# A fused mLSTM, trilinear mixture and Mish mixture: the Mish by ScalarE's own function in two reads of a bank

## The chip, the cores and the metric

One NeuronCore of a Trainium2 chip runs one program. The metric is the device time of one execution in microseconds (us).

## What is computed

Three stages follow one another. An mLSTM attention over 768 steps (2 batches, 8 heads, 40 columns a head) gives 1536 tokens of 320 numbers. The first mixture is `((x @ w1) * (x @ w2)) @ w3 @ w_out` with 1024 inner columns. The second is this, with 2048 inner columns:

```
h = x @ w_in                                                   # 1536 x 320 @ 320 x 2048
sp = np.where(h > 20.0, h, np.log1p(np.exp(np.minimum(h, 20.0))))
g = h * np.tanh(sp)                                            # Mish of h
out = g @ w_out                                                # 2048 x 320
```

The weights arrive as float64. Every product is made from a high and a low part of each operand, three matmuls for one.

## The kernel before

The tokens are handled in three blocks of 512. Inner columns go in tiles of 128, so that a block has 8 tiles in the first mixture and 16 in the second; there are 24 and 48 tiles in all.

**Order.** No loop runs as written. Each step is a node (`Work.add`, L57) with an engine, a due time, a length, the nodes that it needs and the buffers that it takes. `Work.run` (L79) plays this through once while the program is built: on a free engine the nodes that can start within a slack (`s_pe`, `s_act`, `s_dve`, `s_pool` in `TUNE`, L30) of the earliest are compared, and the one that is due first is issued. The order that comes out is fixed in the program, engine by engine. While TensorE has nothing to do before the attention's end, the planner puts in products without a use (`keep_warm`, L365, tile psz); `w0n` of them stand at the start, and the attention's units below `warm` have four each (two in `S_`, two in `Y`).

**Attention.** Twelve units (`add_unit`, L371). Node E, the exponents of a unit, takes one of NW = 3 places named w, which Y of an earlier unit frees (L521). S needs E of its unit and Y of the unit `ahead` before it (L524).

**Weights.** 80 pieces of up to 128 x 384 (`add_piece`, L271), in one fixed order: w1 and w2 (16), w_out of the first mixture (8), w3 (24), the first half of the second mixture's w_out (8, "wo2"), its w_in (16, "wi"), the rest of wo2 (8). A piece is loaded by SyncE's queue; ScalarE takes the magnitude (`mag`, L285); VectorE clamps and joins the words (L289, L293, L298, L303); ScalarE writes the high part (`hi`, L308); GpSimd subtracts for the low part (`lo`, L311, by the helper in L211). There are NF = 5 places f, each held from `mag` to `lo`, and NRAW = 4 places for the loads. From the 17th piece on, `hi` waits for the attention's end (the node `late`); that of a wi piece waits for the product of the third block whose weights lie in its place.

**First mixture.** For each tile two products A and B (L756, L764) of eight matmuls with 512 columns (`mm320`, L742), then Ph, Pl, and X1 (eight matmuls of 512, L778). After a block's last X1, X1l (L814) writes the input of the second mixture. w3 @ w_out is made beforehand (node W, L714).

**Second mixture**, `add_second`, L833. H (L837) is eight matmuls of 512 columns into a bank. Then, for each tile of 128 x 512:

- He, L841: the bank is copied to h, by ScalarE for the first 18 tiles (`he_act`), by VectorE for the other 30.
- Hm, L848, VectorE: u = min(h, 20). Hx, L851, ScalarE: exp.
- G, L907, ScalarE, for two tiles at a time (`GRP`): Ln of both, Tanh of both, with a table load before each pair.
- gm, L854: u = u * h. gh, L857: the high part. gl, L861: the low part. All three are VectorE's.
- O (L865): four times three matmuls of 320 columns into four banks that collect over the 16 tiles of a block. After a block's last O four VectorE copies and four DMAs write its rows (L879).

H of a tile needs its wi piece, X1l of its block and the last W (L887). It can write its bank when He of the tile that had the bank is done. O needs gl and its wo2 piece.

Of the kernel before, what the change touches and what calls it, by code (L numbers as in the profile page):

```python
# [10 lines left out]
F32 = mybir.dt.float32  # L11
F32R = mybir.dt.float32r
# [4 lines left out]
# numbers of buffers  # L17
NRAW = 4
NF = 5
# [6 lines left out]
NUH = 22  # L26
NG_ = 3
GRP = 2
# where the streams of work stand in the order
TUNE = dict(  # L30
    s_pe=0.21, s_act=0.25, s_dve=0, s_pool=0.02, warm=5, ahead=6, w0n=10, he_act=18, a0=132.2, ap=2.52,
    a_ld=-24.1, e_e=289.88, e_s=231.89, e_r=475.63, rb=6, g_ld=-373.09, o_1=-239.57, o_2=520.41, c_ld=-47.15,
    c_wo=548.73, cp_wo=0.032, p0=141.8, pp0=6.543, c_12=-449.5, w0=-140.23, wp=0.004, t_0=-366.73,
    c_w3=-109.65, p1=-597.93, pp1=0.013, p2=-192.0, pp2=621.703, x0=337.71, x_p=-433.57, x1=51.37, x2=-134.49,
    xp=0.002, c_o2=449.63, cp_o2=0.01, c_wi=511.67, c_o3=121.71, m0=987.19, mp0=0.005, mp=1.376, m_o=15.52,
    m_g=228.41, m_t=218.91,
)

# the magnitudes of float32 as the high words of float64, read as float32
# [4 lines left out]
class Work:  # L44
    """Orders the work of the engines: nodes with what they depend on, the places that they take and how long they
    are thought to last; on a free engine the node that is due first comes next."""
# [3 lines left out]
    TABLE = 1.3  # L50
    WINDOW = 3.4133
# [27 lines left out]
    def run(self, t0, fill=None):  # L79
# [15 lines left out]
        def place_of(takes, got):  # L95
            """the place of a list that is free first, or None if none is known to be"""
# [13 lines left out]
        while left:  # L110
# [65 lines left out]
def kernel(  # L176
# [69 lines left out]
    # places of 2 KiB in each partition, the first of them from the start  # L246
# [22 lines left out]
    pieces = []  # L269

    def add_piece(due, lead, width, loads, outs, takes=(), gates=()):  # L271
        """outs: functions that give the tiles of the high and the low part, in the places that takes names"""
# [37 lines left out]
        def low():  # L310
# [4 lines left out]
        add_node(("mag", n), "ACT", due - 4, 0.41 * e, mag, [("load", n), ("mag", n - 1)],  # L315
                 [(places("f", NF), [("lo", n)])])
# [8 lines left out]
    def cols_loads(w, ft):  # L325
        """128 columns of a matrix with 384 rows"""
# [28 lines left out]
    # the factors of the exponents, whose rows are high and low parts of 16 rows of gates each  # L355
# [4 lines left out]
    def load_rows(dst, src, u):  # L360
        """the rows of a unit, all heads of one time step side by side"""
# [3 lines left out]
    def keep_warm(n):  # L365
        """products without a use: the tensor engine's clock falls when its array has little to do"""
# [4 lines left out]
    def add_unit(u, due):  # L371
# [10 lines left out]
        def ld_qk():  # L382
            """the columns of a unit, the heads in pairs at partitions 0 and 64"""
# [137 lines left out]
        node("E", "PE", -K["e_e"], 0.87, E, [("lb", int(c > 0)), ("rb", c), ("E", u - 1)],  # L521
             [at("dw"), at("dw"), (places("w", NW), [("Y", u), ("vw", u)])])
        node("dw", "ACT", -K["e_e"] + 1, 0.96, dw, [("E", u)], table=["exp"])
        node("S", "PE", -K["e_s"], 1.75 + wl, S_, [("ld_qk", u), ("E", u), ("Y", u - K["ahead"])], [at("wg"), at("wg")], warm=wl)  # L524
        node("wg", "DVE", -3, 1.2, wg, [("S", u), ("dw", u), ("vw", u)])
        if c > 0:
            node("I", "PE", -2, 0.87, inter, [("ld_qk", u), ("st", u - B), ("rb", c)],
# [8 lines left out]
        node("Y", "PE", 0, 1.75 + wl, Y, [("wg", u), ("ld_kv", u)], [at("cb")], warm=wl)  # L536
# [5 lines left out]
        node("X", "PE", 3, 0.33, X, [("xo", u)], [at("Xl")], warm=0.0)  # L542
# [25 lines left out]
    def start():  # L568
        G = B * H
        # they stand where the activations come later; the rows of the gates eight times, those of sixteen at 32 n used  # L570
# [37 lines left out]
        def part(c0, c1):  # L608
            """the gates of some chunks: what the exponentials are made of"""
# [93 lines left out]
    def add_w3(i, due, due_c):  # L703
# [30 lines left out]
        add_node(("W", i), "PE", due, 0.406 * n, W,  # L734
# [17 lines left out]
    def add_first(kb, ft, due, due_x):  # L752
# [43 lines left out]
        add_node(("A", i), "PE", due, 1.72, A, [("lo", n1), ("A", i - 1), *units], [(MM if kb == NBLK - 1 else MM1, [("Ae", i)])])  # L796
        add_node(("Ae", i), "ACT", due + 1, 0.48, Ae, [("A", i)], [(ZA, [("Ph", i), ("Pl", i)])])
        add_node(("B", i), "PE", due + 1, 1.72, Bp, [("lo", n2), ("A", i), ("B", i - 1)], [(MM if kb == NBLK - 1 else MM1, [("Be", i)])])
# [4 lines left out]
        add_node(("X1", i), "PE", due_x, 1.72, X1, [("Pl", i), ("Wl", ft), ("X1", i - 1), ("late",)],  # L803
                 [(XB, [("X1l", kb)])] * 3 if ft == 0 else [])

        if ft == KF1 - 1:
# [17 lines left out]
            add_node(("X1h", kb), "ACT", due_x + 1, 1.45, X1h, [("X1", i), *mine], [(places("z", 1, 19), [("X1l", kb)])])  # L824
            add_node(("X1l", kb), "DVE", due_x + 2, 3.0, X1l, [("X1h", kb)])

# [1 line left out]
    NT = NBLK * KF2  # L828
    UH = places("z", NUH, 34 - NUH)
# [3 lines left out]
    def add_second(i, due):  # L833
# [7 lines left out]
        def He():  # L841
            t["u"], t["h"] = z_slot("u"), z_slot("h")
            if i < K["he_act"]:
                nc.scalar.copy(t["h"], t["ps"])
            else:
                nc.vector.tensor_copy(out=t["h"], in_=t["ps"])

        def Hm():  # L848
            nc.vector.tensor_scalar_min(out=t["u"], in0=t["h"], scalar1=20.0)  # L849

        def Hx():  # L851
            nc.scalar.activation(out=t["u"], in_=t["u"], func=AF.Exp)  # L852

        def gm():  # L854
            tt(nc.vector, t["u"], t["u"], t["h"], mult)

        def gh():  # L857
            t["gh"] = z_slot("gh").bitcast(F32R)
            nc.vector.tensor_copy(out=t["gh"], in_=t["u"])
# [19 lines left out]
        def out_rows(j):  # L879
# [5 lines left out]

        g = i // GRP
        add_node(("H", i), "PE", due, 1.73, Hp, [("lo", wi_n[ft]), ("X1l", kb), ("H", i - 1), ("W", KC * NC3 - 1)],  # L887
                 [(MM, [("He", i)])])
        uh = (UH, [("gl", i)])
# [11 lines left out]
        if end:  # L901
            takes = [(places("z", 4), [])] * 4
# [115 lines left out]
```

## Time and profile before

| | |
|---|---|
| median of three runs | 475.64 us (474.4 to 475.76) |
| span of the profiled execution, first to last instruction | 478.8 us |
| TensorE matmuls busy | 456.2 us (95%), 2490 instructions |
| VectorE busy | 399.6 us (83%) |
| ScalarE busy | 295.8 us (62%) |
| GpSimd busy | 127.7 us (27%) |
| chain that ended last, shares of the span | TensorE 63%, VectorE 19%, issue 7%, ScalarE 6% |

The profile is of one other execution; the page gives no time for it besides its span, which lies 3.2 us above the median of the runs. The granted clock is a share of full speed: 1.00 is TensorE's level of 2.4 GHz, 0.50 the one of 1.2 GHz. A matmul that waits in TensorE's pipeline counts as busy, so a busy TensorE can still be one at half its clock.

### The profile page before, as it was taken

The page shows a single profiled execution, that of the slowest core. Times are in us where ns is not written, and L with a number is a line of the kernel's source. Part 1 is how long each engine was busy: PE and PEld are TensorE (multiplying, and loading weights), DVE is VectorE, ACT ScalarE, POOL GpSimd, SP SyncE. Part 2 cuts the span into 40 slices and gives each one's busy share as a digit, 9 for nine tenths or more (in the row PEclk, how much of TensorE's full clock was granted, in tenths as well). Part 3 has the DMA queues.
Part 4 walks back from the last instruction along what each step waited for, and adds up shares of the span by engine and source line. Part 5 has one row for each costly group of instructions (what it writes and reads, how often), then busy time and mean ns, then how long its engine had stood idle before and what let it go on. Part 6 is the DMA issues. An engine that isn't in the chain of part 4 may idle for free.

```text
span 478.8 us, 7146 instructions
## 1 busy us (share of the span) xinstructions
PE 456.2 (95%) x2490; PEld 391.3 (82%) x2490; DVE 399.6 (83%) x809; ACT 295.8 (62%) x513; POOL 127.7 (27%) x141
## 2 busy tenths in 40 slices
PE   6999899899899999999999998987999999999997
PEld 4777788788787798988888886776887889999996
DVE  5988996998969668777698886999599988878874
ACT  7453245423226542244355649997799899999990
POOL 3345264452245222232212221226241100000000
PEclk9669655958979999999999999989899999999999
DMA  7915454443412332233323332324120000001001
GB/s 215 288 53 161 149 172 139 124 126 94 126 34 88 120 111 88 89 93 93 98 60 120 100 100 67 100 73 115 50 82 1 27 30 0 1 1 56 0 2 55
DMA packets 31828, 41.93 MB, mean 88 GB/s; under 512 B 2160, under 2 KB 25968, under 8 KB 31792
## 3 DMA queue, kind: packets, MB, share of 16 engines
q1 hardware_dynamic: 31792, 41.48, 28.5%
q8 instruction: 19, 0.31, 0.3%
q14 instruction: 17, 0.14, 0.1%
HBM read 39.50 MB, written 1.97 MB: 87 GB/s over the span
## 4 chain that ended last, share of the span: by engine, by line
PE 63%; DVE 19%; issue 7%; ACT 6%; POOL 2%; DMA 1%; SPq 1%; POOLq 0%; DVEq 0%; ACTq 0%
PE pso L874 12%; PE psh L747 9%; PE psa L747 8%; PE psb L747 7%; PE psw L721 6%; PE psY L471 4%; DVE f L298 3%; PE psS L422 2%; DVE f L289 2%; DVE f L303 2%; PE psz L369 2%; PE psx L788 2%; PE psx L789 2%; PE psx L787 2%; POOL wil L211 2%
## 5 line engine op out<-in xcount | busy, mean ns | idle before, releaser
L747 PE MATMUL psh<-hs,wih 128*128 128x512 f32 x144 | 57.4, 399 | 0.0
L747 PE MATMUL psh<-hs,wil 128*128 128x512 f32 x144 | 49.5, 398 | 3.1 <-POOL wil L211 3.1
L289 DVE TENSOR_SCALAR f<-f 128x384 f32<-128x384 f32 (+2 forms) x80 | 36.8, 463 | 14.0 <-ACT f L285 13.7
L303 DVE SCALAR_TENSOR_TENSOR f<-raw,f 128x384 int32<-128x384 int32 (+2 forms) x80 | 47.0, 592 | 1.0
L285 ACT ACTIVATE f<-raw 128x384 f32<-128x384 f32 (+2 forms) x80 | 41.5, 524 | 10.2 <-DMA raw<-in_w_dram 5.7
L298 DVE SCALAR_TENSOR_TENSOR f<-raw,f 128x384 int32<-128x384 int32 (+2 forms) x80 | 46.7, 589 | 0.9
L874 PE MATMUL pso<-wo,gh 128*128 128x320 f32 x192 | 42.6, 310 | 0.0
L211 POOL TENSOR_TENSOR th<-f,th 128x384 fp32r<-128x384 f32 (+1 forms) x24 | 23.6, 984 | 61.7 <-ACT th L308 51.6
L211 DVE TENSOR_TENSOR u<-u,h 128x512 f32<-128x512 f32 x48 | 35.1, 746 | 4.9 <-ACT u L911 4.9
L747 PE MATMUL psh<-ls,wih 128*128 128x512 f32 x96 | 38.4, 400 | 0.0
L211 DVE TENSOR_TENSOR gl<-u,gh 128x512 fp32r<-128x512 f32 x48 | 32.7, 686 | 4.9 <-PE pso L874 4.2
L747 PEld LDWEIGHTS psh<-hs,wil 128*128 128x128 f32 x144 | 27.7, 193 | 9.5 <-POOL wil L211 3.6
L293 DVE TENSOR_SCALAR f<-f 128x384 int32<-128x384 int32 (+2 forms) x80 | 34.2, 434 | 1.1
L471 PEld LDWEIGHTS psY<-kv,w 128*128 128x128 f32 x192 | 33.6, 256 | 1.5 <-DVE w L211 0.2
L874 PEld LDWEIGHTS pso<-wo,gh 128*128 128x128 f32 x192 | 32.6, 188 | 1.5 <-issue 0.4
L874 PE MATMUL pso<-wo2h,gl 128*128 128x320 f32 x96 | 30.8, 320 | 3.0 <-DVE gl L211 3.0
L747 PE MATMUL psa<-hs,w12h 128*128 128x512 f32 x72 | 30.4, 422 | 3.1 <-DVE hs L211 2.1
L471 PE MATMUL psY<-kv,w 128*128 128x41 f32 x192 | 33.3, 337 | 0.1
L308 ACT CAST th<-f 128x384 fp32r<-128x384 f32 (+1 forms) x24 | 11.5, 480 | 35.3 <-DVE f L303 23.9
L852 ACT ACTIVATE u<-u 128x512 f32<-128x512 f32 x48 | 28.9, 624 | 5.9 <-DVE u L849 5.6
L211 POOL TENSOR_TENSOR wil<-f,wih 128x384 fp32r<-128x384 f32 x16 | 21.5, 1356 | 41.0 <-ACT wih L308 41.0
L747 PEld LDWEIGHTS psh<-hs,wih 128*128 128x128 f32 x144 | 27.8, 193 | 5.0 <-ACT wih L308 0.2
(137 smaller groups left out, 1250.6 us busy)
## 6 DMA issues: line engine op xcount, KB each, us to landing
raw<-in_w_dram SPq DMA_DIRECT2D x32, 384.0 KB
raw<-in_w_out_dram SPq DMA_DIRECT2D x24, 320.0 KB
raw<-in_w_in_dram SPq DMA_DIRECT2D x16, 384.0 KB
kv<-in_kv_dram SPq DMA_DIRECT2D x12, 324.0 KB
qk<-in_qk_dram SPq DMA_DIRECT2D x24, 160.0 KB
raw<-in_w_dram SPq DMA_DIRECT2D x8, 256.0 KB
sg<-in_o_gate_dram SPq DMA_DIRECT2D x12, 160.0 KB
out_dram<-yo SPq DMA_DIRECT2D x12, 160.0 KB
```

The lines of the kernel that those rows point to most:

```text
L211: return eng.tensor_tensor(out=o, in0=a, in1=b, op=op)
L285: nc.scalar.activation(out=t["f"].bitcast(F32), in_=t["raw"][:, :, 1].bitcast(F32), func=AF.Abs)
L289: nc.vector.tensor_scalar(out=ff, in0=ff, scalar1=HI_MIN, scalar2=HI_MAX, op0=ALU.max, op1=ALU.min)
L293: nc.vector.tensor_scalar(out=f, in0=f, scalar1=3, scalar2=0x3FFFFFFF, op0=ALU.logical_shift_left, op1=ALU.bitwise_and)
L298: nc.vector.scalar_tensor_tensor(out=f, in0=t["raw"][:, :, 1], scalar=-0x40000000, in1=f, op0=ALU.bitwise_and, op1=ALU.bitwise_or)
L303: nc.vector.scalar_tensor_tensor(out=f, in0=t["raw"][:, :, 0], scalar=29, in1=f, op0=ALU.logical_shift_right, op1=ALU.bitwise_or)
L308: nc.scalar.copy(t["h"], t["f"].bitcast(F32))
L471: nc.tensor.matmul(ps[:, h * VW:(h + 1) * VW], lhsT=t["w"][:, h, :], rhs=t["v"][:, h, :], start=True, stop=True)
L721: nc.tensor.matmul(ps, lhsT=t[a][:, c * 128:(c + 1) * 128], rhs=wo[b], start=(c0 + c + s == 0), stop=(c0 + c == KC - 1 and s == 2))
L747: nc.tensor.matmul(ps, lhsT=a, rhs=b, start=(n == 0), stop=(n == len(seq) - 1))
L852: nc.scalar.activation(out=t["u"], in_=t["u"], func=AF.Exp)
L874: nc.tensor.matmul(ps, lhsT=t[a][:, sl], rhs=wo[b], start=(ft == 0 and n == 0), stop=(ft == KF2 - 1 and n == 2))
```

## The change

The second mixture's Mish comes from one ScalarE function. It reads the bank of H twice: `Mh` writes the high part directly (the output type rounds), `Mu` writes the full value, and VectorE's gl subtracts. He, Hm, Hx, G, gm and gh go, with their places. The magnitude of the 32 pieces of the second mixture's weights goes from ScalarE to VectorE, as a bit mask. H now waits for the last B, not for the last W. Lengths in the planner and all of `TUNE` are new; the planner lengthens VectorE's nodes by 1.12. Comments that the diff drops are left out here.

```
 TUNE = dict(
-    s_pe=0.21, s_act=0.25, s_dve=0, s_pool=0.02, warm=5, ahead=6, w0n=10, he_act=18, a0=132.2, ap=2.52,
-    a_ld=-24.1, e_e=289.88, e_s=231.89, e_r=475.63, rb=6, g_ld=-373.09, ...
+    s_pe=0.264, s_act=0.45, s_dve=0, s_pool=1.05, warm=4, ahead=4, w0n=2, a0=127.44, ap=2.22,
+    a_ld=-1.845, e_e=592.82, e_s=226.84, e_r=512.42, rb=7, g_ld=-322.28, ...
...
+    SHARED = 1.12
...
+            if e == "DVE":
+                last *= self.SHARED
...
-    def add_piece(due, lead, width, loads, outs, takes=(), gates=()):
+    def add_piece(due, lead, width, loads, outs, takes=(), gates=(), abs_act=True):
...
         def mag():
             t["f"] = slot(cv, "f", [128, 384], I32)[:, 0:width]
-            nc.scalar.activation(out=t["f"].bitcast(F32), in_=t["raw"][:, :, 1].bitcast(F32), func=AF.Abs)
+            if abs_act:
+                nc.scalar.activation(out=t["f"].bitcast(F32), in_=t["raw"][:, :, 1].bitcast(F32), func=AF.Abs)
+            else:
+                nc.vector.tensor_single_scalar(out=t["f"], in_=t["raw"][:, :, 1], scalar=0x7FFFFFFF, op=ALU.bitwise_and)
...
-        node("E", "PE", -K["e_e"], 0.87, E, ...
+        node("E", "PE", -K["e_e"], 0.92, E, ...
-        node("S", "PE", -K["e_s"], 1.75 + wl, S_, ...
+        node("S", "PE", -K["e_s"], 1.25 + wl, S_, ...
...
-    UH = places("z", NUH, 34 - NUH)
+    GP, UP, YP = places("z", 16), places("z", 4, 16), places("z", 4, 20)
...
-        def He(): ...
-        def Hm(): ...
-        def Hx(): ...
-        def gm(): ...
-        def gh(): ...
+        def Mh():
+            t["gh"] = z_slot("gh").bitcast(F32R)
+            nc.scalar.activation(out=t["gh"], in_=t["ps"], func=AF.Mish)
+
+        def Mu():
+            t["u"] = z_slot("u")
+            nc.scalar.activation(out=t["u"], in_=t["ps"], func=AF.Mish)
...
-        add_node(("H", i), "PE", due, 1.73, Hp, [("lo", wi_n[ft]), ("X1l", kb), ("H", i - 1), ("W", KC * NC3 - 1)],
-                 [(MM, [("He", i)])])
+        add_node(("H", i), "PE", due, 1.82, Hp, [("lo", wi_n[ft]), ("X1l", kb), ("H", i - 1), ("B", NBLK * KF1 - 1)],
+                 [(MM, [("Mu", i)])])
+        gp = (GP, [("O", i)])
+        add_node(("Mh", i), "ACT", due + 2, 0.62, Mh, [("H", i)], [gp], table=["mish"])
+        add_node(("Mu", i), "ACT", due + 2, 0.62, Mu, [("Mh", i)], [(UP, [("gl", i)])], table=["mish"])
+        add_node(("gl", i), "DVE", due + 3, 0.69, gl, [("Mu", i), ("gl", i - 1)], [gp])
...
-        add_node(("O", i), "PE", due + K["m_o"], 1.63, O, [("gl", i), ("lo", wo2_n[ft]), ("O", i - 1)], takes)
-        if last:
-            ...
+        add_node(("O", i), "PE", due + K["m_o"], 1.78, O, [("gl", i), ("lo", wo2_n[ft]), ("O", i - 1)], takes)
```

The lengths of W, A, B, X1, I, Y and X in the planner change in the same way, and `abs_act=False` stands in the three calls that make wo2 and wi pieces.

## Rows read from the trace of the kernel before

**Rows 1.** Busy time by stage (windows of the span): stretch in us from the span's start, its length, then busy us and number of instructions of TensorE's matmuls (PE), its weight loads (PEld), VectorE (DVE), ScalarE (ACT) and GpSimd (POOL), the granted clock, the DMA share and GB/s. The four stretches are the attention, the first mixture, the first part of the second mixture, and its rest.

```profile
0.00:137.95 137.95, 128.45 (x816) 105.61 (x817) 120.21 (x259) 56.76 (x109) 56.63 (x76) 0.75 0.49 146
137.95:283.18 145.23, 144.22 (x700) 122.74 (x699) 115.17 (x228) 67.62 (x150) 42.76 (x45) 1.00 0.30 92
283.18:384.59 101.41, 92.63 (x444) 78.33 (x442) 90.45 (x183) 90.55 (x148) 28.28 (x21) 0.95 0.23 69
384.59:475.51 90.92, 90.91 (x534) 84.64 (x534) 73.26 (x140) 80.92 (x108) 0.00 (x0) 1.00 0.02 8
```

**Rows 2.** The chain of work that ended last, in order of time, two neighbouring pieces of the last stage: start, us, what.

```profile
450.79 1.77 PE pso L874 x12
452.56 1.81 PE psh L747 x8
```

**Rows 3.** The same stretch 283.18 to 384.59 for the instructions of one tile alone, in this order psh (a tile of the second mixture, first product), pso (its second product), psb and psx (the last of the first mixture). The columns are those of rows 1, engines without work left out.

```profile
283.18:384.59 101.41, 58.07 (x232) 44.80 (x231) 6.82 (x10) 9.99 (x18) 0.95 0.23 69
283.18:384.59 101.41, 33.55 (x195) 30.94 (x195) 1.68 (x4) 0.95 0.23 69
283.18:384.59 101.41, 1.98 (x8) 1.50 (x8) 0.69 (x1) 0.95 0.23 69
283.18:384.59 101.41, 2.98 (x9) 1.54 (x8) 1.87 (x3) 1.65 (x3) 0.95 0.23 69
```

**Rows 4.** TensorE's matmuls in order of time (start, us, engine, line, operation, tile, shapes, count, and in brackets the idle time before and what ended it).

```profile
295.90 0.50 PE L787 MATMUL psx<-ph,w 128*128 128x512 f32 x1 [1.66 <-ACT ph L773]
...
334.49 0.73 PE L747 MATMUL psh<-hs,wil 128*128 128x512 f32 x2 [3.14 <-POOL wil L211]
```

**Rows 5.** Busy time of 5 us behind the second of these waits, columns as in rows 1.

```profile
335.00:340.00 5.00, 5.00 (x19) 4.09 (x19) 4.15 (x8) 1.96 (x4) 1.63 (x2) 0.66 0.25 69
```

**Rows 6.** ScalarE in order of time, columns as in rows 4.

```profile
289.99 1.28 ACT L909 ACT_TABLE_LOAD   x1
...
295.24 0.61 ACT L773 CAST ph<-a 128x512 fp32r<-128x512 f32 x1
```

**Rows 7.** The costliest groups of instructions, by shape: line, engine, operation, tiles, shapes, count | busy us, mean ns of one | idle us before them.

```profile
L211 DVE TENSOR_TENSOR u<-u,h 128x512 f32<-128x512 f32 x48 | 35.1, 746 | 4.9 <-ACT u L911 4.9
...
L211 DVE TENSOR_TENSOR gl<-u,gh 128x512 fp32r<-128x512 f32 x48 | 32.7, 686 | 4.9 <-PE pso L874 4.2
...
L909 ACT ACT_TABLE_LOAD x24 | 30.8, 1283 | 0.2
L911 ACT ACT_TABLE_LOAD x24 | 30.8, 1283 | 0.4
...
L852 ACT ACTIVATE u<-u 128x512 f32<-128x512 f32 x48 | 28.9, 624 | 5.9 <-DVE u L849 5.6
...
L909 ACT ACTIVATE u<-u 128x512 f32<-128x512 f32 x48 | 27.7, 625 | 0.3
L911 ACT ACTIVATE u<-u 128x512 f32<-128x512 f32 x48 | 27.7, 624 | 0.3
L285 ACT ACTIVATE f<-raw 128x384 f32<-128x384 f32 x48 | 26.4, 553 | 5.7 <-DMA raw<-in_w_dram 5.7
...
L849 DVE TENSOR_SCALAR u<-h 128x512 f32<-128x512 f32 x48 | 22.2, 465 | 1.4 <-ACT h L844 0.8
...
L859 DVE CAST gh<-u 128x512 fp32r<-128x512 f32 x48 | 21.0, 449 | 0.2
L846 DVE COPY h<-psh 128x512 f32<-128x512 f32 x30 | 20.6, 686 | 8.3 <-PE psh L747 7.7
...
L844 ACT COPY h<-psh 128x512 f32<-128x512 f32 x18 | 10.0, 578 | 2.3 <-PE psh L747 2.2
```

**Rows 8.** VectorE in order of time, columns as in rows 4: one weight piece, and one instruction of a later piece.

```profile
289.53 0.36 DVE L289 TENSOR_SCALAR f<-f 128x384 f32<-128x384 f32 x1 [1.14 <-ACT f L285]
289.93 0.36 DVE L293 TENSOR_SCALAR f<-f 128x384 int32<-128x384 int32 x1
...
290.54 0.55 DVE L298 SCALAR_TENSOR_TENSOR f<-raw,f 128x384 int32<-128x384 int32 x1
291.12 0.56 DVE L303 SCALAR_TENSOR_TENSOR f<-raw,f 128x384 int32<-128x384 int32 x1
...
326.30 1.17 DVE L289 TENSOR_SCALAR f<-f 128x384 f32<-128x384 f32 x1
```

**Rows 9.** All instructions that write the low part of a second-mixture weight (tile wil): shortest/median/longest ns, first and last start.

```profile
L211 POOL TENSOR_TENSOR wil<-f,wih x16: 1016/1110/4260, 274.1 to 335.4; 128x384 fp32r<-128x384 f32 x16
```

**Rows 10.** VectorE's clamp of a weight piece (line 289) by stage, one a piece: stretch, length, busy us and count, clock, DMA share, GB/s.

```profile
0.00:137.95 137.95, 7.64 (x21) 0.75 0.49 146
...
283.18:384.59 101.41, 9.50 (x20) 0.95 0.23 69
```

**Rows 11.** Three stretches of the attention, columns as in rows 1.

```profile
32.00:52.00 20.00, 18.34 (x156) 13.83 (x155) 16.63 (x34) 8.27 (x19) 10.45 (x12) 1.00 0.43 130
52.00:83.00 31.00, 31.00 (x162) 26.58 (x161) 26.52 (x61) 12.42 (x22) 13.44 (x18) 0.50 0.51 150
...
97.00:110.00 13.00, 13.00 (x51) 10.42 (x50) 11.79 (x23) 3.26 (x6) 5.19 (x6) 0.50 0.30 92
```

**Rows 12.** TensorE in the attention, two of the products without a use (tile psz), columns as in rows 4.

```profile
41.25 0.50 PE L369 MATMUL psz<-causal,identr 128*128 128x512 f32 x1
...
62.79 0.77 PE L369 MATMUL psz<-causal,identr 128*128 128x512 f32 x1
```

More of the change, by code (lines that the diff above doesn't have):

```diff
@@ L314, in add_piece @@
                  bytes=width * 1024)
-        add_node(("mag", n), "ACT", due - 4, 0.41 * e, mag, [("load", n), ("mag", n - 1)],
-                 [(places("f", NF), [("lo", n)])])
+        add_node(("mag", n), "ACT" if abs_act else "DVE", due - 4, (0.41 if abs_act else 0.35) * e, mag,
+                 [("load", n), ("mag", n - 1)], [(places("f", NF), [("lo", n)])])
         add_node(("clamp", n), "DVE", due - 3, 0.27 * e, clamp, [("mag", n)])
@@ L732, in Wl @@
             tt(nc.vector, w[:, 512 + R:640], tr[r][:, R0:DM], w[:, 512:512 + R].bitcast(F32), sub)
-        add_node(("W", i), "PE", due, 0.406 * n, W,
+        add_node(("W", i), "PE", due, 0.444 * n, W,
                  [("lo", w3_n[i]), ("W", i - 1), *[("lo", wo_n[c0 + c]) for c in range(n)]],
@@ L823, in add_first @@
             mine = [(x, kb * KF1 + f) for x in "AB" for f in range(KF1)]
-            add_node(("X1h", kb), "ACT", due_x + 1, 1.45, X1h, [("X1", i), *mine], [(places("z", 1, 19), [("X1l", kb)])])
+            add_node(("X1h", kb), "ACT", due_x + 1, 1.45, X1h, [("X1", i), *mine], [(places("z", 1, 33), [("X1l", kb)])])
             add_node(("X1l", kb), "DVE", due_x + 2, 3.0, X1l, [("X1h", kb)])
     NT = NBLK * KF2
-    UH = places("z", NUH, 34 - NUH)
+    GP, UP, YP = places("z", 16), places("z", 4, 16), places("z", 4, 20)
     acc = {}
@@ L884, in out_rows @@
             nc.sync.dma_start(out=out[t0:t0 + T, :], in_=y)
-        g = i // GRP
-        add_node(("H", i), "PE", due, 1.73, Hp, [("lo", wi_n[ft]), ("X1l", kb), ("H", i - 1), ("W", KC * NC3 - 1)],
-                 [(MM, [("He", i)])])
-        uh = (UH, [("gl", i)])
-        add_node(("He", i), "ACT" if i < K["he_act"] else "DVE", due + 2, 0.48 if i < K["he_act"] else 0.6, He, [("H", i)],
-                 [uh, (UH, [("gm", i)])])
-        add_node(("Hm", i), "DVE", due + 2.5, 0.34, Hm, [("He", i)])
-        add_node(("Hx", i), "ACT", due + 3, 0.52, Hx, [("Hm", i)], table=["exp"])
-        last = i % GRP == GRP - 1 or i == NT - 1
-        add_node(("gm", i), "DVE", due + K["m_g"], 0.6, gm, [("G", g)])
-        gp = (places("z", 2 * NG_, 4), [("O", i)])
-        add_node(("gh", i), "DVE", due + K["m_g"], 0.34, gh, [("gm", i), ("X1l", NBLK - 1)], [gp])
-        add_node(("gl", i), "DVE", due + K["m_g"], 0.6, gl, [("gh", i), ("gl", i - 1)], [gp])
+        add_node(("H", i), "PE", due, 1.82, Hp, [("lo", wi_n[ft]), ("X1l", kb), ("H", i - 1), ("B", NBLK * KF1 - 1)],
[4 more added lines that the diff above has]
+        add_node(("gl", i), "DVE", due + 3, 0.69, gl, [("Mu", i), ("gl", i - 1)], [gp])
         end = ft == KF2 - 1
@@ L901, in add_second @@
         if end:
-            takes = [(places("z", 4), [])] * 4
-        add_node(("O", i), "PE", due + K["m_o"], 1.63, O, [("gl", i), ("lo", wo2_n[ft]), ("O", i - 1)], takes)
-        if last:
-            grp = range(g * GRP, i + 1)
-            def G():
-                for n in grp:
-                    nc.scalar.activation(out=mt[n]["u"], in_=mt[n]["u"], func=AF.Ln, bias=1.0)
-                for n in grp:
-                    nc.scalar.activation(out=mt[n]["u"], in_=mt[n]["u"], func=AF.Tanh)
-            add_node(("G", g), "ACT", due + K["m_t"], 1.04 * len(grp), G, [("Hx", n) for n in grp],
-                     table=["ln", "exp"])
+            takes = [(YP, [])] * 4
+        add_node(("O", i), "PE", due + K["m_o"], 1.78, O, [("gl", i), ("lo", wo2_n[ft]), ("O", i - 1)], takes)
     with tc.manual_schedule():
@@ L940 @@
             wo2_n[i] = add_piece(K["c_o2"] + K["cp_o2"] * i, K["c_ld"], DM, rows_loads(w_out2, i),
-                                 outs_of(lambda: late["wo"], f"wo{i}", "wo2", DM), gates=[("W", KC * NC3 - 1)])
+                                 outs_of(lambda: late["wo"], f"wo{i}", "wo2", DM), gates=[("W", KC * NC3 - 1)], abs_act=False)
         dues = []
```

46 lines of the change are left out of this document (14 added, 32 removed).

## The prediction

> **What bounds the kernel now.** I read busy time by stage first, because the share of the whole span averages over stages with different limits [rows 1]. From 137.95 us to 283.18 us TensorE is busy for 144.22 of 145.23 us at full clock, and from 384.59 us on for 90.91 of 90.92 us: there only less TensorE work would save time, and the change removes none. Two stretches are left. The attention, up to 137.95 us, has a mean clock of 0.75 and VectorE busy for 120.21 us. The first part of the second mixture, 283.18 to 384.59 us, has TensorE at 92.63 of 101.41 us and a clock of 0.95, while VectorE (90.45 us) and ScalarE (90.55 us) are both about nine tenths busy.
>
> How much does that third stretch lose? The chain of waits gives the price of undisturbed work: 1.81 us for eight matmuls of 512 columns, 1.77 us for twelve of 320, that is 0.226 us and 0.1475 us each [rows 2]. The stretch holds 232 matmuls of H, 195 of O and eight each of the last B and the last X1 (the ninth psx record begins before it) [rows 3]. 248 x 0.226 + 195 x 0.1475 = 56.1 + 28.8 = 84.9 us. The stretch lasts 101.41 us, so **16.5 us** are lost, to idle time and to the half clock behind it. That is the most that the second mixture can give back.
>
> Who causes the loss is seen in TensorE's own waits [rows 4]. At 295.90 us the last X1 had waited 1.66 us for Ph, and in ScalarE's order Ph stands behind a whole group G: a table load begins at 289.99 us and Ph only at 295.24 us [rows 6]. At 334.49 us H had waited 3.14 us for the low part of a weight. After that wait the clock is 0.66 over 5 us, another 1.7 us of full-speed work [rows 5]. The other waits of the stretch are of the same two kinds, late elementwise work and late weights.
>
> **The change, part by part.** *ScalarE, off the path at the end.* Removed: 48 table loads (30.8 + 30.8 us), the 18 copies of He (10.0), exp (28.9), ln (27.7) and tanh (27.7), together 155.9 us [rows 7]. Added: 96 Mish reads. The trace shows no Mish. The nearest rows bound it: 0.578 us for a copy of the same tile from a bank, 0.624 us for a table function on it [rows 7]; I take 0.62, being a table function, so 60 us. The 32 magnitudes that leave (0.553 us for the wide ones [rows 7]) are about another 17 us. So a tile needs 1.24 us of ScalarE where its H and O take 1.81 + 1.77 = 3.58 us of TensorE: hidden. The cover ends at 1.79 us a read.
>
> The Trainium skill (ScalarE: Activation LUTs, What ACT_TABLE_LOAD costs) gives 186 ns + 0.833 ns an element for any function, which is 0.613 us for 512 elements and 59 us for the 96 reads. The exp, ln and tanh rows agree within 2%, and no row shows Mish.
>
> *VectorE.* Removed: gm 35.1, He 20.6, Hm 22.2, gh 21.0, together 98.9 us [rows 7]. gl stays at 0.686 us a tile. Added: 32 masks. Bounds: 0.36 us, a one-source bit operation on a piece, and 0.55 us, one that reads the same strided words but has a second source [rows 8]. I take 0.36, the row with the same count of sources: 12 us, at most 18. Within the third stretch the account is this. He takes 6.82 us there [rows 3]; Hm of 29 tiles (232 / 8) 13.5; gm and gh of 16 tiles (195 / 12) 19.1. So 39.4 us go, and 20 pieces [rows 10] bring at most 11 us. VectorE needs some 62 us where TensorE needs 84.9. It stops being a bound.
>
> *Weight supply.* One piece costs VectorE 0.36 + 0.36 + 0.55 + 0.56 = 1.83 us [rows 8], with the mask 2.2 us. A tile of the first block needs one wi piece, half of the tiles need a narrower wo2 piece (five sixths of the cost, 1.8 us), and gl: 2.2 + 0.9 + 0.69 = 3.8 us against 3.58 us of TensorE. Sixteen tiles want 61 us of VectorE against 57 us. The low part of the first wi piece starts at 274.1 us [rows 9], nine us ahead of the stretch, and that start more than covers the four. Moreover the magnitude no longer hops through ScalarE, where it waited behind G: the clamp of one piece stood 1.14 us idle for it [rows 8].
>
> *H waits for the last B.* An H that the order had ahead of that B now comes behind it, where it can fill the wait for the last Ph. The work only changes place: nothing, and the cover is that wait itself. The places for u, h, gh and gl change too; H can run eight tiles ahead of O (16 places for gh and gl), 14 us of H, more than the wait for X1l. Nothing.
>
> *Attention.* Its work is the same. VectorE handles 21 pieces there [rows 10]: 16 with places of their own and five that fill the NF places until the attention ends; the diff leaves that limit alone, and all 21 keep ScalarE's magnitude. `ahead` 6 to 4 adds no wait, since S needs E and E already needs a w place that Y three units earlier frees. `rb` 6 or 7 is the same for six chunks. `warm` 4 takes four products from the fifth unit, two like that at 41.25 us and two like that at 62.79 us, some 1.3 us of TensorE [rows 12]. The shorter `w0n` is made up by the planner's own filling. What does change is the order, through the new due times, slacks and lengths. SP's loads keep their sequence; their places depend on the pieces, so they move with the order. The price of an order can't be read from a trace of another one. Its ends are these: the shorter of the two half-clock stretches shown, 97 to 110 us [rows 11], raised to full clock saves at most 6.5 us; the full-clock stretch of 32 to 52 us fallen to half costs at most its busy time again, 18.3 us [rows 11]. Without a reason for either I take 0.
>
> *Sum.* Of the 16.5 us I leave one wait like the first of the two with as much again in half clock, 3.5 us; its ends are 0 and 8. So 13 us go. Against the span of the profiled execution: 478.8 - 13 = 465.8 us. That span stands 3.2 us above the median of the runs, so the runs should show 475.64 - 13 = 462.6 us; I say **462.5 us**.
>
> **The rivals.** *A, forecast,* 457 to 468 us: chance 0.53.
>
> *B, late weights keep half of it.* When GpSimd works, a clamp took 1.17 us and not 0.36, and a low part took 4.26 us where the shortest took 1.016 [rows 8, 9]. If the new masks meet the low parts in this way, waits like the 3.14 us one stay, each with about 1.7 us of half clock behind it; two of them make 9.7 us, the gain is 7 us and the time 469 us. For it: the mask sits on the very path that ends at such a low part. Against it: Hm and gh, 96 one-source operations, leave the same stage. Chance 0.15.
>
> The Trainium skill (SBUF — State Buffer, SBUF: two separate sides) says that VectorE, in an operation that uses two ports or reads two operands in SBUF, and GpSimd lock a shared pair of ports for a whole instruction. By that rule the mask can block and be blocked, which speaks for B; the rows above are of that kind, and no row shows the mask itself.
>
> *C, slower.* The new order lets the clock fall in the attention. Place: 32 to 52 us, held at full clock among the products without a use, of which the change takes some away; price up to 18.3 us [rows 11], time 462.5 + 18.3 = 480.8 us. From 13 us on it ends above 475.6. For it: 52 to 83 us already runs at 0.50. Against: part of that stretch waits on VectorE, which a slower clock would leave hidden. Chance 0.13.
>
> *D, a better attention.* One half-clock stretch goes: 6.5 us and the 3.5 us that I left: 452.5 us. Chance 0.14.
>
> *E, the function does not do what it says.* A Mish read that costs all three functions that it replaces, 1.87 us [rows 7], makes ScalarE's 3.74 us a tile the pace: 48 x 0.16 = 8 us of the gain go, 470 us; beyond 1.93 us a read nothing is left. Chance 0.05.
>
> **How the numbers follow.** About 0.3% (1.4 us) is what a measurement of this kernel can tell from no change. A, B and D are faster, 0.82 together. C is slower, 0.13. E, whose time hangs on how dear the read is, I count as the 0.05 for no change. The range takes in A and B and most of D and stops short of C's price: 452 to 474 us, leaving out C and the edges of D and E, about 0.2. The likeliest case's own range is 457 to 468 us.
>
> **What would show each step.** Right: no table loads between the second mixture's tiles; Mish rows near 0.6 us; VectorE about 85 us less busy and ScalarE over 100; from the last B to the end TensorE at clock 1.00 with waits of under 4 us in sum. The last B, the last X1 and all H and O cost 2 x 1.81 + 48 x 3.58 = 175.5 us, and the time from the first of them to the last O should be near that. Wrong: a wait for wil of over 3 us (B); an attention that ends, with the same matmuls done, later than 137.95 us by more than 6 us (C) or earlier by more than 4 (D); Mish rows above 1 us (E). If the gain is right but the stage before 283 us moved by as much, the forecast was right by luck.

## The result: 15.5 us faster, and the profile after

The changed kernel takes **459.54 us** (median of 4 runs, 458.88 to 460.07), the kernel before 475.02 us (4 runs, 471.91 to 475.76): a ratio of 0.966, 95% interval 0.963 to 0.970, or 15.5 us. The forecast was 462.5 us. The profiled execution after has a span of 457.1 us and took 459.14 us.

First the same amount of work in both traces. The stretch below holds all of H and O and 16 more matmuls of 512 columns (before, the last B and the last X1; after, the last two X1), and ends with the last O; the two rows hold the same number of matmuls (977). Busy time by window, kernel before, columns as in [rows 1]:

```profile
283.18:475.51 192.33, 183.53 (x977) 162.97 (x975) 163.71 (x322) 171.47 (x255) 28.28 (x21) 0.97 0.13 40
```

And the kernel after, that work alone, then three stages (the attention, and the two parts of the second mixture):

```profile
275.83:453.50 177.67, 176.20 (x977) 159.40 (x975) 87.82 (x163) 64.16 (x121) 25.62 (x20) 1.00 0.13 41
...
0.00:133.60 133.60, 119.49 (x843) 98.49 (x843) 118.31 (x261) 57.34 (x111) 56.06 (x76) 0.86 0.50 150
...
275.83:331.00 55.17, 53.74 (x269) 46.16 (x268) 51.81 (x101) 28.83 (x55) 21.60 (x16) 1.00 0.33 100
331.00:453.50 122.50, 122.46 (x710) 113.24 (x708) 36.01 (x63) 35.32 (x66) 4.03 (x5) 1.00 0.04 14
```

The second mixture fell from 192.33 to 177.67 us: **14.7 us**. Half of it is idle time of TensorE (192.33 - 183.53 = 8.8 us before, 1.5 after), half the same matmuls at full clock (183.53 to 176.20 us; clock 0.97 to 1.00). VectorE halved in that stretch, ScalarE fell to three eighths.

The spans differ by 21.7 us (478.8 and 457.1), and 7.3 of these lie ahead of that stretch (283.18 - 275.83). Most of the 7.3 is not the change. The first profile of before is of a slow execution, with a granted clock of 0.918 over the span where a second profile has 0.949; that second one (span 472.5 us, before_again below) ends its last B 6.4 us sooner and loses the same in the second mixture. Against it the span fell by 15.4 us, which is what the runs show.

What TensorE still waits for, the four largest of its waits in sum (engine, tile, line, releaser; us, times, longest), after:

```profile
PE psS L427 <- DMA qk<-in_qk_dram: 6.2, 4, 3.2
PE psz L374 <- ACT causal L598: 3.2, 1, 3.2
PE psa L752 <- DVE w L212: 3.1, 1, 3.1
PE psh L752 <- POOL wil L212: 1.3, 1, 1.3
```

Only the last lies in the second mixture. It answers to the 3.14 us wait of [rows 4]; the one for Ph is gone. Here it is in order of time by engine, after GpSimd and VectorE around it (columns as in [rows 4]; the engine is each line's third field):

```profile
290.76 7.34 POOL L212 TENSOR_TENSOR wil<-f,wih 128x384 fp32r<-128x384 f32 x3 [5.52 <-ACT wih L313]
...
294.51 1.45 DVE L212 TENSOR_TENSOR gl<-u,gh 128x512 fp32r<-128x512 f32 x1
295.88 1.35 DVE L303 SCALAR_TENSOR_TENSOR f<-raw,f 128x384 int32<-128x384 int32 x1
297.15 1.17 DVE L290 TENSOR_SCALAR f<-raw 128x384 int32<-128x384 int32 x1
...
296.87 0.73 PE L752 MATMUL psh<-hs,wil 128*128 128x512 f32 x2 [1.33 <-POOL wil L212]
```

All low parts of these weights, columns as in [rows 9], and the 5 us behind the wait, columns as in [rows 1]:

```profile
L212 POOL TENSOR_TENSOR wil<-f,wih x16: 1011/1062/4652, 265.9 to 318.1; 128x384 fp32r<-128x384 f32 x16
```

```profile
297.00:302.00 5.00, 5.00 (x24) 4.19 (x25) 5.00 (x12) 2.86 (x6) 2.10 (x2) 1.00 0.26 79
```

Three low parts run one after another, the first of them the longest of all, 4.65 us, and the last VectorE operations beside them are stretched too: the new mask (line 290) takes 1.17 us here, where its two groups below have means of 0.40 and 0.36. Behind the wait the clock stays at 1.00; [rows 5] had 0.66.

The groups that changed (columns as in [rows 7]), after:

```profile
L848 ACT ACTIVATE gh<-psh 128x512 fp32r<-128x512 f32 x48 | 28.8, 600 | 82.0 <-PE pso L867 71.1 <-PE psh L752 10.9
L852 ACT ACTIVATE u<-psh 128x512 f32<-128x512 f32 x48 | 28.3, 595 | 0.0
...
L848 ACT ACT_TABLE_LOAD x1 | 1.3, 1283 | 0.0
...
L212 DVE TENSOR_TENSOR gl<-u,gh 128x512 fp32r<-128x512 f32 x48 | 36.3, 761 | 66.6 <-PE pso L867 66.1 <-ACT u L852 0.5
...
L290 DVE TENSOR_SCALAR f<-raw 128x384 int32<-128x384 int32 x16 | 6.5, 403 | 0.0
...
L290 DVE TENSOR_SCALAR f<-raw 128x320 int32<-128x320 int32 x16 | 5.8, 363 | 0.0
```

One table load for Mish in place of 48, Mish at 0.60 us a read, and both engines now idle for 66 to 71 us until an O frees a place: there TensorE sets the pace. That idle time lies behind the first part of the second mixture, where VectorE is still busy for 51.81 of 55.17 us. The page's totals: ScalarE 183.4 us busy (before 295.8), VectorE 329.7 (399.6), TensorE 435.6 (456.2).

### The profile page after: what moved, and what is told of

The parts are those of the page before. It is cut to its first block, busy times and chain, and to the rows that moved or that the text cites. A ratio compares the mean times of both kernels' runs of the same rounds, so it can differ in the third digit from the quotient of the medians.

```text
span 457.1 us, 6822 instructions
## 1 busy us (share of the span) xinstructions
PE 435.6 (95%) x2494; PEld 376.5 (82%) x2494; DVE 329.7 (72%) x667; ACT 183.4 (40%) x368; POOL 128.4 (28%) x141
## 4 chain that ended last, share of the span: by engine, by line
PE 44%; issue 3%; DVE 2%; POOL 2%; ACT 0%; POOLq 0%
PE pso L867 18%; PE psh L752 16%; PE psa L752 2%; POOL wil L212 2%; PE psb L752 2%; PE psx L792 1%; PE psx L794 1%; PE psx L793 1%; DVE f L303 1%; DVE f L298 1%; PE psx L796 1%; PE psx L797 1%; PE psw L726 0%; DVE f L308 0%; DVE f L294 0%
## 5 line engine op out<-in xcount | busy, mean ns | idle before, releaser
L212 DVE TENSOR_TENSOR gl<-u,gh 128x512 fp32r<-128x512 f32 x48 | 36.3, 761 | 66.6 <-PE pso L867 66.1
L848 ACT ACTIVATE gh<-psh 128x512 fp32r<-128x512 f32 x48 | 28.8, 600 | 82.0 <-PE pso L867 71.1
L298 DVE TENSOR_SCALAR f<-f 128x384 int32<-128x384 int32 (+2 forms) x80 | 42.4, 535 | 1.2
L212 POOL TENSOR_TENSOR th<-f,th 128x384 fp32r<-128x384 f32 (+1 forms) x24 | 26.2, 1093 | 56.0 <-ACT th L313 47.0
L294 DVE TENSOR_SCALAR f<-f 128x384 f32<-128x384 f32 (+2 forms) x80 | 32.5, 412 | 7.0 <-ACT f L288 6.4
L726 PE MATMUL psw<-woh,th 128*128 128x320 f32 x128 | 29.4, 313 | 0.8 <-POOL th L212 0.6
L867 PE MATMUL pso<-wo2h,gh 128*128 128x320 f32 x96 | 29.8, 310 | 0.0
L867 PE MATMUL pso<-wo2l,gh 128*128 128x320 f32 x96 | 29.7, 309 | 0.0
L867 PE MATMUL pso<-wo,gl 128*128 128x320 f32 x96 | 29.7, 309 | 0.0
L752 PE MATMUL psb<-hs,w12h 128*128 128x512 f32 x72 | 29.0, 403 | 0.0
```

What stands on the lines that cost most here:

```text
L212: return eng.tensor_tensor(out=o, in0=a, in1=b, op=op)
L294: nc.vector.tensor_scalar(out=ff, in0=ff, scalar1=HI_MIN, scalar2=HI_MAX, op0=ALU.max, op1=ALU.min)
L298: nc.vector.tensor_scalar(out=f, in0=f, scalar1=3, scalar2=0x3FFFFFFF, op0=ALU.logical_shift_left, op1=ALU.bitwise_and)
L726: nc.tensor.matmul(ps, lhsT=t[a][:, c * 128:(c + 1) * 128], rhs=wo[b], start=(c0 + c + s == 0), stop=(c0 + c == KC - 1 and s == 2))
L752: nc.tensor.matmul(ps, lhsT=a, rhs=b, start=(n == 0), stop=(n == len(seq) - 1))
L848: nc.scalar.activation(out=t["gh"], in_=t["ps"], func=AF.Mish)
```

## The experiments

The change is a function and an order at once, and the function relieves two engines at once. So I asked three things: is it the function or the order; is it VectorE's passes or ScalarE's loads; how far does TensorE cover the reads. Each kernel below was run four times or more, beside the kernel before on the same chip (medians 475.6, 476.5 and 475.6 us in the three sittings). "Loss" is, in its profile, the time from the end of the last B to the end of the last O less the matmuls left then at the prices of [rows 2]; it is 17.1 us before and 2.4 us after.

| kernel | median us | ratio to before (95%) | loss us |
|---|---|---|---|
| before (second profile) | 474.43 | 0.996 (0.992 to 1.000) | 17.2 |
| after | 459.54 | 0.966 (0.963 to 0.970) | 2.4 |
| order_alone | 479.15 | 1.009 (1.006 to 1.011) | 23.4 |
| function_alone | 461.31 | 0.972 (0.968 to 0.977) | 3.0 |
| mag_scalar | 481.63 | 1.015 (1.010 to 1.019) | 25.9 |
| mag_copy | 458.37 | 0.963 (0.957 to 0.969) | 1.8 |
| vector_back | 487.28 | 1.023 (1.016 to 1.030) | 30.1 |
| vector_planned | 487.81 | 1.027 (1.021 to 1.032) | 31.1 |
| tables_back | 496.41 | 1.041 (1.033 to 1.049) | 38.2 |
| tables_planned | 462.43 | 0.972 (0.968 to 0.976) | 6.4 |
| mish_three | 464.41 | 0.976 (0.972 to 0.980) | 7.2 |
| mish_five | 512.42 | 1.076 (1.069 to 1.084) | 54.6 |
| mish_five_near | 482.83 | 1.016 (1.010 to 1.021) | 24.9 |

Set function_alone and order_alone against before's median of their sitting and the first profile's loss, and the others against after: time and loss change by the same within 1.5 us, in order_alone within 2.8. So what these edits cost or gain lies in the main in the second mixture.

### Function or order

**before_again** is the kernel before, with the same code, for a second profile.

> The kernel before once more, for a second profile of it. Theory one (the gain lies in the waits of the second mixture): from the last B to the last O 15 to 18 us are lost again, and the 4 to 6 us by which the first profile was longer than the median of the runs lie ahead of that, in the attention. Theory two (the loss of the second mixture is itself a chance of one execution): the loss there differs by 4 us or more between the two profiles.

Its span was 472.5 us, its loss 17.2 us, its last B ended at 287.73 us where the first profile had 294.13. So the loss in the second mixture is steady, and what comes ahead of it is not.

**order_alone** keeps the second mixture of before, with its own due numbers and with the magnitudes on ScalarE, behind the new numbers and lengths of all that comes ahead of it.

```diff
-            nc.scalar.activation(out=t["gh"], in_=t["ps"], func=AF.Mish)
...
+            nc.vector.tensor_scalar_min(out=t["u"], in0=t["h"], scalar1=20.0)
...
+            nc.scalar.activation(out=t["u"], in_=t["u"], func=AF.Exp)
...
```

> The new numbers and lengths of the planner for all that comes ahead of the second mixture, with the second mixture, its numbers and its magnitudes as before. Theory one (the function takes the waits away): 472 to 476 us, 0 to 3 us off the kernel before. Theory two (the order brings the gain, the function only moves work): 460 to 465 us.

**function_alone** is the reverse: two Mish reads, their places and the mask, with all numbers and lengths of before, and H waiting for the last W as before.

```diff
-    s_pe=0.264, s_act=0.45, s_dve=0, s_pool=1.05, warm=4, ahead=4, w0n=2, a0=127.44, ap=2.22,
+    s_pe=0.21, s_act=0.25, s_dve=0, s_pool=0.02, warm=5, ahead=6, w0n=10, he_act=18, a0=132.2, ap=2.52,
...
```

> The Mish reads, their places and the mask, with every number and length of the planner as before. Theory one: 459 to 463 us, TensorE's waits from the last B on under 5 us in sum. Theory two: 470 us or more, with waits of over 8 us left there.

The order alone is 0.9% slower than before, outside both ranges. Its largest wait, in the view of waits:

```profile
PE psh L755 <- ACT h L852: 15.1, 4, 4.4
```

The function alone takes 461.31 us, 14.3 us less than before on the same chip, and loses 3.0 us. **The gain is the function's, together with the mask** (the next runs part the two). The new order is worth another 0.6 points of the ratio, and the two intervals overlap: between nothing and some 5 us, not told apart here.

### Where the magnitude is taken

**mag_scalar** leaves all in place but takes every magnitude on ScalarE again, as before. The planner isn't told: the instructions keep the order that was made with these 32 magnitudes on VectorE.

```diff
-            if abs_act:
+            if True:
```

> The changed kernel with the 32 magnitudes of the second mixture's weights on ScalarE again, in the same sequence of instructions. Theory one (VectorE and ScalarE are both off the path now, so the mask's engine does not matter): 459 to 461 us. Rival (the hop through ScalarE delays the weights): 463 us or more, with waits for wil of over 3 us. The other rival (the masks lock with GpSimd and hold up the low parts): 458 us or less.

It ran at 481.63 us, slower than the kernel before, and none of the theories had named the reason. Two of its groups, then ScalarE in order of time:

```profile
L848 ACT ACT_TABLE_LOAD x15 | 19.2, 1283 | 0.3
L288 ACT ACT_TABLE_LOAD x15 | 19.2, 1283 | 0.3
```

```profile
300.40 1.28 ACT L288 ACT_TABLE_LOAD   x1
301.70 0.55 ACT L288 ACTIVATE f<-raw 128x384 f32<-128x384 f32 x1
302.15 0.50 ACT L313 CAST wih<-f 128x384 fp32r<-128x384 f32 x1
302.66 1.28 ACT L848 ACT_TABLE_LOAD   x1
303.96 0.60 ACT L848 ACTIVATE gh<-psh 128x512 fp32r<-128x512 f32 x1
```

Abs and Mish are not served by one table set here: a magnitude that follows a Mish read has a table load before it, and the next read has one for Mish. That is 30 loads, 38 us of ScalarE in the stretch where weights and tiles meet. In the kernel before, the same magnitudes stood among exp, ln and tanh and had no load of their own (none at line 285). The Trainium skill (ScalarE: Activation LUTs, Table sets: the hidden batching unit) says that abs is in every set; this trace, with its 30 loads, says otherwise for Mish's.

**mag_copy** tests that reason: the same 32 pieces on ScalarE, by a copy. It leaves out the absolute value, so its weights are not those of the computation; only its time is of use.

```diff
-                nc.vector.tensor_single_scalar(out=t["f"], in_=t["raw"][:, :, 1], scalar=0x7FFFFFFF, op=ALU.bitwise_and)
+                nc.scalar.copy(t["f"].bitcast(F32), t["raw"][:, :, 1].bitcast(F32))
```

> The 32 magnitudes again on ScalarE in the same sequence, but as a copy and not as Abs (so the signs of the second mixture's weights stay in, and the output is not the reference's). Theory one (Abs and Mish do not share a table set, and the 30 loads between them made the 20 us of the run before): 459 to 462 us, no table loads between the tiles. Rival (the place in ScalarE's order, behind work that waits, is what costs): 470 us or more without the loads.

458.37 us, and six table loads in all, as after. So in this order it doesn't matter which engine takes the magnitude; that it is not Abs between Mish reads is worth 22 us. What the Abs would cost in an order made for its loads was not tried; the loads of tables_planned, below, all but vanish in such an order.

### VectorE's passes or ScalarE's loads

**vector_back** puts passes of the kind that VectorE lost back ahead of each gl's subtraction, 94 us by the page's total, and they change no value.

```diff
+            nc.vector.tensor_scalar_min(out=t["u"], in0=t["u"], scalar1=1e30)
+            tt(nc.vector, t["u"], t["u"], t["u"], ALU.max)
+            nc.vector.tensor_scalar_max(out=t["u"], in0=t["u"], scalar1=-1e30)
+            if i >= 18:
+                tt(nc.vector, t["u"], t["u"], t["u"], ALU.max)
```

> The changed kernel with VectorE's removed passes put back as passes that leave u as it is: per tile two one-source operations and one of two sources ahead of gl, for the tiles from 18 on one more; the planner's lengths as they are. Some 93 us of VectorE. Theory A (VectorE's load made the waits of the first block): 464 to 470 us, waits for gl or wil of 4 us and more. Theory B (ScalarE alone made them): 459 to 462 us.

**tables_back** puts the 48 loads back, by a one-element exp after every second tile.

```diff
+            if i % 2:
+                nc.scalar.activation(out=tab_o, in_=tab_i, func=AF.Exp)
```

> The changed kernel with a small exp after every second tile, so that 48 table loads of 1.28 us (62 us of ScalarE) come back, and nothing else. Theory A (VectorE's load made the waits): 459 to 462 us. Theory B (ScalarE's loads made them, in front of Ph and of the high parts): 464 us or more, with TensorE waiting for u or for wih.

487.28 and 496.41 us: vector_back above both of its ranges, tables_back as its theory B had it, and both far above the kernel before, which carried loads of both kinds at once. But these kernels run in an order made without the added work. So the next two tell the planner of it, with eight places each for gh and gl and the reads in tile order.

```diff
-    GP, UP, YP = places("z", 16), places("z", 4, 16), places("z", 4, 20)
+    GP, GL, UP, YP = places("z", 8), places("z", 8, 8), places("z", 4, 16), places("z", 4, 20)
...
-        add_node(("gl", i), "DVE", due + 3, 0.69, gl, ...
+        add_node(("gl", i), "DVE", due + 3, 2.0 if i < 18 else 2.6, gl, ...      (vector_planned)
-        add_node(("Mu", i), "ACT", due + 2, 0.62, Mu, ...
+        add_node(("Mu", i), "ACT", due + 2, 0.62 + 2.7 * (i % 2), Mu, ...        (tables_planned)
```

> VectorE's removed passes put back as in the run vector_back, but with lengths of 2.0 and 2.6 us in the planner, so that the order is made for them; gh and gl get eight places each and the reads keep the tiles' sequence. Theory A (an order made for the load hides it where only ScalarE is light): 459 to 463 us. Theory B (VectorE alone accounts for a good part of the 15 us that the change gave): 466 to 474 us. Above 480 us the order would not be what cost the 28 us of vector_back.

> The 48 table loads put back as in the run tables_back, but with 2.7 us a pair in the planner; places and sequence as in vector_planned. Theory A (ScalarE's loads can be hidden by an order made for them where VectorE is light): 459 to 463 us. Theory B (they alone account for a good part of the 15 us): 466 to 474 us. Above 485 us the order is not what cost the 37 us of tables_back.

VectorE's passes cost the same in an order made for them, 487.81 us. That is 14 us above the range of the theory of VectorE, and above the 480 us beyond which the order was not to blame for the cost of vector_back. Its windows (columns as in [rows 1]) and TensorE's largest waits for gl and weights:

```profile
300.00:320.00 20.00, 13.32 (x72) 11.23 (x70) 19.62 (x38) 6.33 (x12) 9.22 (x6) 1.00 0.34 107
320.00:340.00 20.00, 18.56 (x83) 16.33 (x84) 19.00 (x36) 7.01 (x13) 2.80 (x3) 0.83 0.10 28
340.00:360.00 20.00, 11.36 (x47) 9.36 (x46) 19.14 (x44) 4.01 (x8) 5.66 (x4) 0.77 0.17 55
```

```profile
PE pso L872 <- DVE gl L212: 8.5, 5, 3.7
PE pso L872 <- ACT wo L313: 5.4, 1, 5.4
```

VectorE is busy for 57.8 of 60 us: full. The forecast's account gives the size. A tile of the first block wants 3.8 us of VectorE, and its three passes add 0.44 + 0.75 + 0.51 = 1.7, the mean times of their groups (columns as in [rows 7]):

```profile
L212 DVE TENSOR_TENSOR u<-u 128x512 f32<-128x512 f32 x78 | 58.8, 754 | 2.7
...
L858 DVE TENSOR_SCALAR u<-u 128x512 f32<-128x512 f32 x48 | 24.4, 508 | 1.6
...
L856 DVE TENSOR_SCALAR u<-u 128x512 f32<-128x512 f32 x48 | 20.9, 436 | 12.3 <-ACT u L852 12.3
```

So 16 tiles are 16 x (5.5 - 3.58) = 31 us too long; the loss rose by 28.7. The loads went the other way. In the order made for them they cost 2.9 us. The windows of tables_planned:

```profile
300.00:320.00 20.00, 19.31 (x102) 16.69 (x101) 17.34 (x32) 17.62 (x27) 5.46 (x5) 1.00 0.30 95
320.00:340.00 20.00, 19.79 (x109) 17.61 (x108) 18.38 (x39) 16.91 (x27) 4.98 (x5) 1.00 0.21 66
```

ScalarE is at 86% there and TensorE still at 98%. **So VectorE's passes are what neither order tried here makes up for; ScalarE's loads matter only where the order has not made room for them.** Two limits: of ScalarE's relief only the loads were put back (its total is 247.5 us, before 295.8), and vector_planned puts more on VectorE than the kernel before carried, since the passes come back and the masks stay (420.7 us in all, before 399.6). Over the same number of matmuls as in the first row of the result, vector_planned has 178.49 us of VectorE where before has 163.71:

```profile
276.73:482.86 206.13, 185.75 (x977) 165.24 (x975) 178.49 (x336) 65.59 (x121) 27.27 (x20) 0.95 0.11 35
```

These 14.8 us go with a loss of 31.1 us against 17.1. That the one makes the other is not shown, and neither is what VectorE's load of before alone would cost in the new kernel. Its own 22 places for u and h are another difference that was not tried.

### How far TensorE covers the reads

**mish_five** and **mish_three** read the bank for u four times and twice instead of once, in the order of after.

```diff
-            nc.scalar.activation(out=t["u"], in_=t["ps"], func=AF.Mish)
+            for _ in range(4):        # mish_three: range(2)
+                nc.scalar.activation(out=t["u"], in_=t["ps"], func=AF.Mish)
```

> The changed kernel with the second Mish read of each tile done four times: five reads, 3.0 us of ScalarE a tile against 3.58 us of TensorE. If the cover is as forecast (it ends where a tile's ScalarE work passes TensorE's): 459 to 464 us, the rest being the first block, where the high parts of the weights come on top. Rival (the latency of a tile's reads counts, not their sum): 470 us or more.

> Three reads a tile, 1.86 us, in the order of the changed kernel. Theory of the loop: a pair takes 2 x 1.86 + 2.1 + 1.8 = 7.6 us against 7.15, 0.4 us on some 20 pairs and a few in the first block: 466 to 474 us. Theory of the share (1.86 beside 3.58 us is hidden): 459 to 462 us.

By engine time both should be hidden: five reads are 3.0 us a tile against 3.58. They cost 52.9 and 4.9 us. The first is far outside the range of the share and in the rival's; mish_three's 464.41 us lies between its two ranges. ScalarE of mish_five in order of time, then two steps of its chain:

```profile
389.19 0.60 ACT L848 ACTIVATE gh<-psh 128x512 fp32r<-128x512 f32 x1 [3.97 <-PE pso L868]
389.68 2.48 ACT L853 ACTIVATE u<-psh 128x512 f32<-128x512 f32 x4
392.06 0.59 ACT L848 ACTIVATE gh<-psh 128x512 fp32r<-128x512 f32 x1
392.54 2.49 ACT L853 ACTIVATE u<-psh 128x512 f32<-128x512 f32 x4
398.84 0.60 ACT L848 ACTIVATE gh<-psh 128x512 fp32r<-128x512 f32 x1 [3.81 <-PE pso L868]
```

```profile
433.75 2.11 PE psh L752 x8
435.86 1.63 PE pso L868 x11
...
443.41 2.14 PE psh L752 x8
```

Behind the first block it is a loop, not a share. The order makes H in pairs and runs them ahead until all gh places are taken. Then the reads of two tiles (5.8 us) wait for an O to free a place, that O waits behind the next H, and that H waits for the bank that the reads free: 5.8 + 3.9 = 9.7 us a pair, where TensorE needs 7.15. The same loop in mish_three:

```profile
402.12 0.60 ACT L848 ACTIVATE gh<-psh 128x512 fp32r<-128x512 f32 x1 [3.90 <-PE pso L868]
...
404.37 1.23 ACT L853 ACTIVATE u<-psh 128x512 f32<-128x512 f32 x2
409.48 0.60 ACT L848 ACTIVATE gh<-psh 128x512 fp32r<-128x512 f32 x1 [3.88 <-PE pso L868]
```

402.12 to 409.48 is 7.4 us: 3.5 of reads and 3.9 of waiting, just over 7.15. The kernel itself, with 2.4 us of reads a pair, stays below it. So both runs give one estimate for this order: behind the first block the cover ends where the reads of two tiles exceed 7.15 - 3.9 = 3.3 us, that is 0.8 us a read. The first block is not parted in this way: from its first H to its last O it took 104 us in mish_five and 80 after, and there the high parts of the weights come on top of the reads.

**mish_five_near** breaks the loop with the five reads kept: O is due close behind its H, so that the two alternate.

```diff
-mp=0.928, m_o=268.95,
+mp=0.928, m_o=3.8,
```

> Five reads a tile as in the run mish_five, but O due some four tiles behind H (m_o 3.8), so that H and O alternate and H no longer runs until the places for gh are full. Theory of the loop (in mish_five a pair of tiles took 9.66 us: reads of two tiles 5.7, one H 2.1, one O 1.8, one behind the other, because the reads waited for the places that O frees): 462 to 472 us, since 3.0 us a tile then lie beside 3.58. Rival (ScalarE's sum with the high parts is what bounds): 495 us or more.

It gives back 29.6 of the 52.9 us, at 482.83 us in neither range. The end runs at full pace, as this part of the chain shows (an H every 3.58 us):

```profile
453.53 1.81 PE psh L752 x8
457.11 1.81 PE psh L752 x8
```

That is the loop theory's half. It missed its range in the first block, where TensorE waits for the reads and for weights whose high parts ScalarE writes among them:

```profile
PE psh L752 <- ACT u L853: 3.7, 5, 2.0
...
PE pso L868 <- ACT wo L313: 3.3, 5, 2.3
...
PE pso L868 <- POOL wo L212: 3.1, 6, 0.5
```

ScalarE is busy for 18.82 of 20 us there (columns as in [rows 1]), as the rival's sum would have it for that block:

```profile
300.00:320.00 20.00, 16.61 (x74) 12.97 (x73) 13.02 (x25) 18.82 (x35) 4.85 (x4) 0.91 0.22 72
```

## Why the prediction was right, step by step

**The stretch.** Right, and for its reason. Of the 16.5 us I let 13 go; 14.7 went. I had left one wait of 1.66 us and as much in half clock; what is left is one wait of 1.33 us at full clock and small gaps. The stretch of 175.5 us of work took 177.67.

**Luck ahead of it?** The text named as luck a gain of which as much lies ahead of 283 us. In the two first profiles 7.3 us did. The second profile of before and function_alone settle it: the function gives 14.3 us with the old order. The order's zero was right within what can be told; order_alone shows that the same numbers can also go with 4 us more, with another second mixture.

**The base.** I took "3.2 us above the median" as a fixed shift of that execution. In the later profiles a run's time is 1.7 to 2.1 us above its span, so that execution was some 5 us longer than the median, by its attention (last X at 139.8 us, 133.5 in the second profile). The shift did no harm because the loss that I counted lies behind it and was the same in both.

**ScalarE, Mish.** 0.60 us a read was forecast as 0.62, the total 112 us less as "over 100". Rival E fell. The step **"The cover ends at 1.79 us a read" was wrong**: it compared busy shares, and in this order the chain through the banks and the gh places ends the cover at about 0.8 us (estimated above from mish_three and mish_five; no dearer read itself was run). E's price, no gain left only beyond 1.93 us, is wrong with it: three reads in place of two, 0.6 us a tile, already took back 4.9 us.

**VectorE.** The masks cost 12.3 us, as said (12). "About 85 us less" was 69.9. Some 7 us of the difference is work that stayed and took longer (gl 36.3 for 32.7 us; clamp and joining of the weights together 168.6 for 165.1). The rest is in the counting: the forecast added groups, while neighbouring rows overlap (the gl shown above ends at 294.51 + 1.45 = 295.96 us, and the next row starts at 295.88) and the page's total counts such time once; the durations of all VectorE instructions, added in the trace, fell from 439.6 to 359.3 us. In the first part VectorE stayed nearly full, as the account of 3.8 us a tile has it; its room lies behind. That its passes can't be put back in the two orders tried is shown by vector_back and vector_planned, at a load above that of before; the forecast had relieved both engines and not asked which.

**The mask's place.** I priced it as 12 us of VectorE and a shorter way for the weights. Its worth is another one: in this order the magnitudes by Abs on ScalarE would have brought 30 table loads and 22 us. The forecast named no such cost.

**B, late weights.** Its mechanism is there: the mask took 1.17 us beside a low part, and a low part up to 4.65 us (shortest 1.011). The Trainium skill's rule of the shared ports (SBUF — State Buffer, SBUF: two separate sides), cited in the prediction, agrees with the mask's row. Its price was too high: one wait of 1.33 us, no half clock.

**C and D.** The attention's end moved from 133.5 us (second profile of before) to 134.5 us for the last product of X: neither. By the sign that the prediction set, against the 137.95 us of the first profile, it would have been D: 843 matmuls were done by 133.60 us. But the kernel before, in its second profile, has done the same 816 as in [rows 1] by 131.50 us:

```profile
0.00:131.50 131.50, 116.93 (x816) 95.66 (x817) 121.74 (x258) 56.08 (x109) 56.31 (x75) 0.84 0.49 153
```

So that sign measured one execution of before. The half-clock stretches of [rows 11] are not fixed either: in the second profile 52 to 83 us has a clock of 0.83 and 97 to 110 us one of 0.99. `ahead` and `rb` put back to 6 give the same instructions in the same order on every engine, so "nothing" is exact there.

## What to carry to other kernels

Price a saving by the stretch in which the bound engine idles or runs at half clock: the 16.5 us lost there bounded the gain, though 180 us of other engines' work went. Whether an engine beside the path is covered is not its busy share against the bound engine's, but the time around the loop through its buffers in the order that is issued. When a new function comes onto ScalarE, look at what else runs there between its calls: one function from another table set can cost more than the change gives, where the order has no room for its loads.

## What the hardware showed that I had not expected

- Abs has a table load before it when it follows Mish (15 of them in mag_scalar), a copy or a cast has none (mag_copy). A switch costs the 1283 ns of the load: in the rows above the next activation starts 1.30 us after the load did (300.40 to 301.70), so nothing but the load is seen at a switch.
- Of the 61.6 us of 48 loads, an order and places made for them hid all but 2.9 us; in the order made without them they cost 36.9 us.
